# Attention with pooled queries, then a tanhshrink FFN: the sums of p in three instead of four rounds on TensorE

## The chip, the cores and the metric

One core of one Trainium2 chip runs the whole program in a single launch. The metric is the device time of the program in microseconds; the time before is the median of three runs.

## What is computed

The inputs are q, k and v of shape (8, 8, 1152, 64), that is 8 batches of 8 heads, and the two weights of an FFN, w_in (512 x 2048) and w_out (2048 x 512). The reference, cut to what matters:

```python
q_pool = q.reshape(B, H, S // 2, 2, D).mean(axis=3)
scores = scale * np.matmul(q_pool, k.transpose(0, 1, 3, 2))
scores = scores - np.max(scores, axis=-1, keepdims=True)
attn = np.exp(scores)
attn = attn / (np.sum(attn, axis=-1, keepdims=True) + 1e-09)
x = np.matmul(attn, v)            # then heads are put side by side: 4608 tokens x 512
h = x @ w_in
g = h - np.tanh(h)
out = g @ w_out
```

The change lies in np.sum(attn), the sum over the 1152 keys of the exponentials p.

## The kernel before, in words

The first half of the program is the attention, the second half the FFN. The attention goes over 32 pairs of heads (4 pairs in each of 8 batches). The two heads of a pair lie in the upper and the lower 64 partitions. A pair is worked in two halves of 288 pooled queries, and a half in 9 key tiles of 128 keys.

For one key tile TensorE makes the scores of both heads (`scores`, line 262): four products of 288 columns per head, with q and k split into a high and a low float32r part and a last product that adds minus the row maximum. ScalarE turns them into p (`p_f`, 128 x 2 x 288). After the ninth tile `pv` (line 285) multiplies all nine p tiles with v.

**The sums of p.** They are not taken on ScalarE but in two steps. GpSimd adds p tiles together (`z_part`, line 277): `z_groups` (line 449) names three groups of key tiles in each half, (0, 1, 2), (3, 4, 5) and (6, 7), and a group becomes one tile `z` with one addition fewer than it has members. The ninth p tile, key tile 8, is left alone. At the end of the second half `z_sums` (line 298) adds over the 128 keys of a tile with products of a 128 x 32 block of ones, in four rounds: first groups one and two, then the lone p tile, then group three. A round is four products, for two halves and two heads, each in its own 32 columns of the array. They go into the free half of the PSUM tile that the product with v fills.

**The row maxima for the next pair.** Between the score products TensorE also makes raw scores of high parts for the following pair (`max_part`, line 217, 15 of them in a pair, nine in the first half of a pair's time and six in the second, which ends with the sums), and VectorE reduces each to maxima (`mx`), 128 x 768 elements at a time. VectorE further makes the low part `lo` of q and k (line 213), and `nm`, `mt`.

**PSUM.** `banks()` (line 172) gives tiles of two banks from a pool of four. Scores, raw scores, the product with v and a small transposition all take their tile there, so that a tile comes free only after the ScalarE or VectorE instruction that reads it.

**The weights.** In the background of each pair one block of 512 weight columns is split into two float32r parts (`w_block`, line 347). That is five VectorE instructions on 128 x 512 elements (the trace names them `w<-w` and `w<-w_raw,w`; two of them are the last before a pair ends, a clip and a bitwise `and`, and three come at the middle of the pair), two of ScalarE and two of GpSimd (`w<-w,w` and `w_hl<-w,w_hl`).

**The order of the work** is written out by hand. Time is counted in units `u`, 36 for a pair (`U`) and 18 for a half (`G`); `add(u, f)` files a piece of work under a unit, and `run(u)` emits it there. Every engine keeps the order of emission (`InOrder`). Inside a pair, with r = u mod 36, the places that matter here are

- r = 35: the last group of `z_part`, `lo` of the pair after the next one, clip and `and` of the weight block; then `pv` and the sums;
- r = 36, that is r = 0 of the next pair: first the copies of the product and of the sums to SBUF, an early `max_part`, then the scores;
- r = 1: the `w_hl` subtraction of the weight block on GpSimd;
- r = 10: `query_sums` (line 201) on GpSimd, the sum `kq` of the two queries that are pooled, for the pair after the next one; its `hi` parts follow on ScalarE at r = 17;
- r = 22: the store of the maxima `m_dram` on SyncE's queue, which waits for VectorE; r = 28: the loads of q and k (`load`, line 185) for the pair after the next two, and the read of the maxima `mb`.

Pieces filed under the same unit keep the order in which they were filed; those of the loop at line 417 come ahead of what is filed while the program runs, so `query_sums` would come ahead of `w_hl` at the same unit, and `load` ahead of the store of the maxima.

```python
units = dict(load=-80, query_sums=-62, hi=-55, lo=-37, load_v=-30)
...
z_groups = {kts[-1]: kts for kts in ((0, 1, 2), (3, 4, 5), (6, 7))}
...
if r // 2 in z_groups:
    add(u + 1, z_part, hf, z_groups[r // 2])
```

Of the kernel before, what the change touches and what calls it, by code (L numbers as in the profile page):

```python
# [43 lines left out]
def kernel(  # L44
# [38 lines left out]
    ones = const.tile([P, 32], F32, name="ones")  # L83
# [51 lines left out]
    t, n = chunks.pop()  # L135
# [4 lines left out]
    with ExitStack() as actx:  # L140
# [10 lines left out]
        pe, act, dve, pool, sp = (InOrder(tc, e) for e in (nc.tensor, nc.scalar, nc.vector, nc.gpsimd, nc.sync))  # L151

        HQ = SQ // 2
# [23 lines left out]
        def add(u, f, *args, at=at):  # L177
            at.setdefault(u, []).append(lambda: f(*args))
# [106 lines left out]
        def pv(u, hf):  # L285

            w, ps = hf.w, banks()
            hf.o = ps[:, 0]
            for kt in range(KT):
                for h in range(2):  # L290
                    pe.matmul(hf.o[64 * h:64 * h + 64, 0:HQ], w.v[:, h, kt], hf.p[kt][:, h], start=(kt == 0),
                              stop=(kt == KT - 1), tile_position=(0, 64 * h))
            add(u + 1, o_out, w, hf, at=first)
            w.halves.append(hf)
            if hf.n == 1:
                z_sums(u, w, ps[:, 1])

        def z_sums(u, w, ps):

            parts = [[*hf.zs[:2], hf.p[-1], hf.zs[2]] for hf in w.halves]  # L300
            for g in range(4):
                for n in range(2):
                    for h in range(2):
                        r = 64 * h + 32 * n
                        pe.matmul(ps[r:r + 32, 0:HQ], ones, parts[n][g][:, h], start=(g == 0), stop=(g == 3), tile_position=(0, r))
            add(u + 1, z_out, u + 1, w, ps, at=first)

        def o_out(w, hf):
# [107 lines left out]

        for pi in range(n_pair):
            u = pi * U
            units = dict(load=-80, query_sums=-62, hi=-55, lo=-37, load_v=-30)
            row, steps = -19, (5, 11)  # L420

            spots = [x for half, us in ((-54, (2, 4, 8, 10, 12, 14, 16)), (-36, (2, 4, 8, 10, 14, 16)))
                     for x in [(early, half)] + [(at, half + i) for i in us]]
            if pi == 0:
                units.update(load=-70, query_sums=-62, hi=-60, lo=-41, load_v=-40)
                spots = [(at, -60 + i) for i in range(15)]
                row, steps = -43, (3, 4)
            if pi == 1:
                units.update(load=-104)
            add(u + units["load"], load, pi)  # L430
            add(u + units["query_sums"], query_sums, pi, dve if pi < 1 else pool)
            for c in range(0, KQ, SQ):
                add(u + units["hi"], hi_part, pi, c, c + SQ)
            add(u + units["lo"], lo_part, pi)
            for i, (when, x) in enumerate(spots):
                add(u + x, max_part, u + x, pi, i // 3, i % 3, at=when)
            add(u + units["load_v"], load_v, pi)
            add(u + row, max_rows, u + row, pi, steps)

        def run(u, at=at):  # L440

            while at.get(u):
                at[u].pop(0)()

        for u in range(min(at), 0):
            run(u, first)
            run(u, early)
            run(u)
        z_groups = {kts[-1]: kts for kts in ((0, 1, 2), (3, 4, 5), (6, 7))}
        for u in range(end + 60):  # L450
            run(u, first)
            run(u, early)
            n, r = divmod(u, G)
            if u < end and r % 2 == 0:
                if r == 0:
                    hf = Half()
# [18 lines left out]
    pe, pool, sp = (InOrder(tc, e) for e in (nc.tensor, nc.gpsimd, nc.sync))  # L475
# [81 lines left out]
    for ci, (t0, n) in enumerate(chunks):  # L557
        x_h, x_l, _ = xs
        po = []
        for fc in range(NF):  # L560
# [3 lines left out]
            load = []  # L564
            if ci + 1 < len(chunks):
# [3 lines left out]
                load = [xs[2][(fc - x) // 3][i] for i, x in ((3, 3), (0, 0), (1, 2), (2, 2)) if (fc - x) % 3 == 0 and 0 <= fc - x < 3 * NP]  # L569
            for f in load:  # L570
                f()
            g = hidden(x_h, x_l, n, fc)
# [44 lines left out]
```

## Time and profile before

| | before |
|---|---|
| median of 3 runs | 1643.94 us (1643.39 to 1645.49) |
| the profiled execution, whole | 1643.04 us |
| its span, first to last instruction | 1641.3 us |
| granted TensorE clock, mean over the span | 0.999 of 2.4 GHz |
| TensorE busy over the span | 1609.8 us (98%) |
| VectorE busy | 1319.6 us (80%) |
| ScalarE busy | 1023.9 us (62%) |
| GpSimd busy | 942.9 us (57%) |

The span is the profiler's time from the first to the last instruction of one execution. The execution itself took 1.74 us more, and 0.90 us less than the median. The attention fills about the first 843 us of the span, the FFN the rest. PE stands for TensorE's products, PEld for its weight loads, DVE for VectorE, ACT for ScalarE, POOL for GpSimd, and SPq for SyncE's queue of DMA issues. A line of 37 only says that the instruction went through the helper that keeps the order. Products are pipelined: a row of many shows from the start of the first to the end of the last, and their ends overlap with what starts next, so the distance of two starts is the better measure.

### The profile page before, as it was taken

The page shows a single profiled execution, that of the slowest core. Times are in us where ns is not written, and L with a number is a line of the kernel's source. Part 1 is how long each engine was busy: PE and PEld are TensorE (multiplying, and loading weights), DVE is VectorE, ACT ScalarE, POOL GpSimd, SP SyncE. Part 2 cuts the span into 40 slices and gives each one's busy share as a digit, 9 for nine tenths or more (in the row PEclk, how much of TensorE's full clock was granted, in tenths as well). Part 3 has the DMA queues.
Part 4 walks back from the last instruction along what each step waited for, and adds up shares of the span by engine and source line. Part 5 has one row for each costly group of instructions (what it writes and reads, how often), then busy time and mean ns, then how long its engine had stood idle before and what let it go on. Part 6 is the DMA issues. An engine that isn't in the chain of part 4 may idle for free.

```text
span 1641.3 us, 32231 instructions
## 1 busy us (share of the span) xinstructions
PE 1609.8 (98%) x12576; PEld 1245.2 (76%) x12576; DVE 1319.6 (80%) x1725; ACT 1023.9 (62%) x1865; POOL 942.9 (57%) x694
## 2 busy tenths in 40 slices
PE   5999999999999999999999999999999999999999
PEld 3667777777777777677778888888888888888898
DVE  7889888888898888888848677777777777777786
ACT  2655656556556565565566666666666666666786
POOL 2778778778787787877854343433434342423332
PEclk9999999999999999999999999999999999999999
DMA  3343444334433344343547110101011111000100
GB/s 141 120 138 108 126 127 136 125 108 138 135 115 125 121 141 126 108 130 133 183 146 268 39 36 21 48 26 52 26 47 31 39 39 39 26 33 20 32 22 27
DMA packets 72665, 147.86 MB, mean 90 GB/s; under 512 B 11136, under 2 KB 36672, under 8 KB 72512
## 3 DMA queue, kind: packets, MB, share of 16 engines
q1 hardware_dynamic: 72512, 145.80, 27.3%
q8 instruction: 99, 1.62, 0.4%
q14 instruction: 54, 0.44, 0.1%
HBM read 109.49 MB, written 36.27 MB: 89 GB/s over the span
## 4 chain that ended last, share of the span: by engine, by line
PE 85%; DVE 13%; issue 1%; ACT 0%; DMA 0%; DVEq 0%; ACTq 0%
PE ps L37 37%; PE ps_h L37 24%; PE ps_o L37 24%; DVE w L37 6%; DVE mx L37 6%; DVE nm L37 0%; DVE lo L37 0%; DMA q_n<-in_q_dram 0%; ACT hi L37 0%; DVE rec L37 0%; DVE kq L37 0%; ACT p_f L37 0%; DVEq L37 0%; ACT x L552 0%; ACT z_s L37 0%
## 5 line engine op out<-in xcount | busy, mean ns | idle before, releaser
L37 DVE TENSOR_REDUCE mx<-ps 128x2 f32<-128x768 f32 x480 | 434.3, 951 | 73.9 <-PE ps L37 73.7
L37 POOL TENSOR_TENSOR g_lo<-g_s,g_hi 128x512 fp32r<-128x512 f32 (+1 forms) x160 | 190.3, 1190 | 483.3 <-ACT g_hi L520 445.2
L37 ACT ACTIVATE p_f<-ps 128x576 f32<-128x576 f32 x576 | 361.7, 650 | 93.6 <-PE ps L37 79.3
L37 POOL TENSOR_TENSOR z<-p_f 128x576 f32<-128x576 f32 x192 | 280.0, 1459 | 154.1 <-ACT p_f L37 154.1
L37 PE MATMUL ps<-hi 64*128 64x288 f32 (+1 forms) x2112 | 316.7, 352 | 23.7 <-DVE mx L37 13.7
L37 PE MATMUL ps_h<-x,wi 128*128 128x512 f32 (+1 forms) x1440 | 318.3, 370 | 0.0
L37 PE MATMUL ps_o<-wo,g_hi 128*128 128x512 f32 x1008 | 311.5, 390 | 0.0
L37 PE MATMUL ps<-p_f,v 128*64 128x288 f32 x2304 | 293.5, 409 | 0.0
L37 PEld LDWEIGHTS ps_h<-x,wi 128*128 128x128 f32 x1440 | 253.1, 188 | 50.5
L37 PEld LDWEIGHTS ps<-hi 64*128 64x128 f32 x2112 | 194.4, 187 | 89.2 <-DVE mx L37 34.6
L37 PEld LDWEIGHTS ps<-p_f,v 128*64 128x64 f32 x2304 | 159.8, 137 | 113.7 <-ACT p_f L37 12.0
L509 ACT ACTIVATE g_u<-ps_h 128x512 f32<-128x512 f32 (+1 forms) x160 | 88.9, 556 | 236.3 <-PE ps_h L37 236.1
L514 DVE SCALAR_TENSOR_TENSOR ps_w<-g_u,ps_h 128x512 f32<-128x512 f32 (+1 forms) x160 | 103.1, 645 | 157.8 <-ACT g_t L510 157.2
L37 PEld LDWEIGHTS ps_o<-wo,g_hi 128*128 128x128 f32 x1008 | 187.6, 188 | 39.2
L37 POOL TENSOR_TENSOR z<-z,p_f 128x576 f32<-128x576 f32 x128 | 194.0, 1516 | 11.8 <-ACT p_f L37 1.9
L37 PE MATMUL ps_o<-wo,g_lo 128*128 128x512 f32 x504 | 196.2, 389 | 0.0
L37 PE MATMUL ps<-lo,hi 64*128 64x288 f32 x1152 | 170.8, 293 | 0.0
L37 PE MATMUL ps<-hi,lo 64*128 64x288 f32 x1152 | 170.7, 293 | 0.0
L37 PE MATMUL ps<-mb,ones_k 64*128 64x288 f32 x1152 | 170.2, 292 | 0.0
L37 ACT ACTIVATE o_s<-ps 128x288 f32<-128x288 f32 x64 | 26.3, 412 | 230.4 <-PE ps L37 230.4
L519 DVE COPY_PREDICATED g_s<-g_m,g_t 128x512 f32<-128x512 int32 (+1 forms) x160 | 115.0, 719 | 17.1 <-DVE g_s L518 0.9
L517 DVE SCALAR_TENSOR_TENSOR ps_w<-g_s,ps_w 128x512 f32<-128x512 f32 (+1 forms) x160 | 102.9, 643 | 16.6 <-DVE ps_w L516 0.5
(68 smaller groups left out, 2399.7 us busy)
## 6 DMA issues: line engine op xcount, KB each, us to landing
q_n<-in_q_dram SPq DMA_DIRECT2D x32, 576.0 KB
kq<-in_k_dram SPq DMA_DIRECT2D x32, 576.0 KB
v<-in_v_dram SPq DMA_DIRECT2D x32, 576.0 KB
x_dram<-o_s SPq DMA_DIRECT2D x32, 288.0 KB
out_dram<-o_s SPq DMA_DIRECT2D x34, 256.0 KB
w_raw<-in_moe_w_in_dram SPq DMA_DIRECT2D x16, 512.0 KB
wi_dram<-w_hl SPq DMA_DIRECT2D x16, 512.0 KB
w_raw<-in_moe_w_out_dram SPq DMA_DIRECT2D x16, 512.0 KB
```

The lines of the kernel that those rows point to most:

```text
L37: ins = self.tc.keep_in_program_order(f(*args, **kwargs))
L509: nc.scalar.activation(u, h, AF.Square)
L514: nc.vector.scalar_tensor_tensor(w, u, -P0, h, op0=ALU.add, op1=ALU.mult)
L517: nc.vector.scalar_tensor_tensor(w, s2, P2, w, op0=ALU.add, op1=ALU.mult)
L519: last = nc.vector.copy_predicated(s1, m.bitcast(I32), th).ins
```

## The change

The ninth p tile joins the third group on GpSimd, and the sums take three rounds of products with ones in place of four. The query sums of a pair are filed nine units sooner (r = 1 in place of r = 10; not for pairs 0 and 1), the loads of q and k six units sooner (r = 22 in place of r = 28; not for pairs 0 and 1).

```diff
         def z_sums(u, w, ps):
 
-            parts = [[*hf.zs[:2], hf.p[-1], hf.zs[2]] for hf in w.halves]
-            for g in range(4):
+            for g in range(3):
                 for n in range(2):
                     for h in range(2):
                         r = 64 * h + 32 * n
-                        pe.matmul(ps[r:r + 32, 0:HQ], ones, parts[n][g][:, h], start=(g == 0), stop=(g == 3), tile_position=(0, r))
+                        pe.matmul(ps[r:r + 32, 0:HQ], ones, w.halves[n].zs[g][:, h], start=(g == 0), stop=(g == 2),
+                                  tile_position=(0, r))
             add(u + 1, z_out, u + 1, w, ps, at=first)
...
-            units = dict(load=-80, query_sums=-62, hi=-55, lo=-37, load_v=-30)
+            units = dict(load=-86, query_sums=-71, hi=-55, lo=-37, load_v=-30)
...
             if pi == 1:
-                units.update(load=-104)
+                units.update(load=-104, query_sums=-62)
...
-        z_groups = {kts[-1]: kts for kts in ((0, 1, 2), (3, 4, 5), (6, 7))}
+        z_groups = {kts[-1]: kts for kts in ((0, 1, 2), (3, 4, 5), (6, 7, 8))}
```

## Rows read from the trace of the kernel before

**Rows 1.** One stretch: busy PE, PEld, DVE, ACT, POOL; clock, DMA share, GB/s.

```profile
400.00:500.00 100.00, 99.27 (x1102) 71.51 (x1100) 89.03 (x94) 60.16 (x107) 79.45 (x52) 1.00 0.40 126
```

**Rows 2.** The page's chain that ended last: share of the span by engine.

```profile
PE 85%; DVE 13%; issue 1%; ACT 0%; DMA 0%; DVEq 0%; ACTq 0%
```

**Rows 3.** Timeline of PE, end of a pair: start, duration (us), instruction.

```profile
391.38 0.94 PE L37 MATMUL ps<-z,ones 128*32 128x288 f32 x12
...
416.62 1.18 PE L37 MATMUL ps<-z,ones 128*32 128x288 f32 x16
417.62 0.67 PE L37 MATMUL ps<-p_f,ones 128*32 128x288 f32 x8
418.10 0.67 PE L37 MATMUL ps<-z,ones 128*32 128x288 f32 x8
418.70 0.57 PE L37 MATMUL ps<-hi 64*128 64x384 f32 x4
...
420.03 0.57 PE L37 MATMUL ps<-hi 64*128 64x384 f32 x4
420.43 0.30 PE L37 MATMUL ps<-lo,hi 64*128 64x288 f32 x2
```

**Rows 4.** Timeline of DVE, same pair's end (in brackets idle, releaser).

```profile
413.33 3.02 DVE L37 TENSOR_TENSOR lo<-kq,hi 128x1728 fp32r<-128x1728 f32 x1
416.27 1.49 DVE L37 TENSOR_SCALAR w<-w 128x512 f32<-128x512 f32 x1
...
417.79 0.43 DVE L37 TENSOR_SCALAR w<-w 128x512 int32<-128x512 int32 x1
419.18 0.96 DVE L37 TENSOR_REDUCE mx<-ps 128x2 f32<-128x768 f32 x1 [0.96 <-PE ps L37]
```

**Rows 5.** Timeline of POOL over the same end of a pair.

```profile
413.12 1.41 POOL L37 TENSOR_TENSOR z<-p_f 128x576 f32<-128x576 f32 x1
414.48 2.99 POOL L37 TENSOR_TENSOR w_hl<-w,w_hl 128x512 fp32r<-128x512 f32 x1
421.06 1.43 POOL L37 TENSOR_TENSOR z<-p_f 128x576 f32<-128x576 f32 x1 [3.59 <-ACT p_f L37]
```

**Rows 6.** Groups of instructions by line: count, busy us, mean ns, idle before.

```profile
L37 PE MATMUL ps<-p_f,ones 128*32 128x288 f32 x256 | 21.4, 406 | 0.0
```

**Rows 7.** Timelines of DVE and POOL at the start of the attention.

```profile
20.78 1.95 DVE L37 TENSOR_TENSOR lo<-kq,hi 128x1728 fp32r<-128x1728 f32 x1
...
32.41 1.63 DVE L37 TENSOR_SCALAR w<-w 128x512 f32<-128x512 f32 x1
...
34.07 1.50 DVE L37 TENSOR_SCALAR w<-w 128x512 int32<-128x512 int32 x1
...
32.01 1.74 POOL L37 TENSOR_TENSOR z<-p_f 128x576 f32<-128x576 f32 x1 [22.93 <-ACT p_f L37]
33.84 1.46 POOL L37 TENSOR_TENSOR z<-z,p_f 128x576 f32<-128x576 f32 x1
35.25 1.58 POOL L37 TENSOR_TENSOR kq<-q_n 128x576 f32<-128x576 f32 x1
```

**Rows 8.** Timeline of PE, the sums of pairs 1 and 2.

```profile
85.47 1.18 PE L37 MATMUL ps<-z,ones 128*32 128x288 f32 x16
...
112.53 1.18 PE L37 MATMUL ps<-z,ones 128*32 128x288 f32 x16
```

**Rows 9.** Timelines of POOL and PE, last pair but one.

```profile
819.73 1.86 POOL L37 TENSOR_TENSOR z<-p_f 128x576 f32<-128x576 f32 x1
821.55 1.73 POOL L37 TENSOR_TENSOR w_hl<-w,w_hl 128x512 fp32r<-128x512 f32 x1
...
820.08 1.18 PE L37 MATMUL ps<-z,ones 128*32 128x288 f32 x16
```

**Rows 10.** Timeline of SyncE's queue over the same pair.

```profile
407.44 0.34 SPq L37 DMA_DIRECT2D q_n<-in_q_dram  x1
...
421.22 1.24 SPq L37 DMA_DIRECT2D wo_dram<-w_hl  x1
```

## The prediction

> **What bounds the kernel now.** I read the table of busy time by stretch first. In a steady stretch of the attention TensorE is busy 99% of the time, VectorE 89% and GpSimd 79%, at the full granted clock [rows 1]. Three engines are nearly full, so it is not enough to know which one is fullest: the reader is to see that work moved from the first to the third has little room. The chain of waits says the same for the whole span: 85% of it lies on TensorE and 13% on VectorE [rows 2]. The place where they meet is the end of a pair, so I then read the timelines of three engines there. On TensorE the sums start at 416.62, and the lone p tile's round lasts from 417.62 to 418.10, 0.48 us, as does the next; the first product of the next pair starts at 418.70. From one pair's sums to the next it is 25.24 us [rows 3]. VectorE works through `lo`, clip and `and` until 418.22, and then waits 0.96 us for TensorE before it makes the first maxima of the next pair at 419.18 [rows 4]. GpSimd ends with the last group of p and `w_hl` at 417.47, and is then idle until 421.06 [rows 5].
>
> **The round that goes.** Four products a pair, two records each: 256 records in 32 pairs [rows 6]. By the distance of starts a round costs 0.48 us [rows 3], so 32 x 0.48 = 15.4 us leave TensorE's queue. That is the most the change can give.
>
> **The additions that come.** One in each half, 64 in all, of 1.43 us when nothing disturbs them [rows 5]: 92 us of GpSimd. A pair has 25.24 us, of which GpSimd is busy 79% [rows 1], 20.1 us; with 2 x 1.43 it is 22.9. They fit, but not without meeting VectorE.
>
> **Turns between VectorE and GpSimd.** With GpSimd idle `lo` takes 1.95 us [rows 7]; beside the additions it takes 3.02 [rows 4]. Rows 7 show how this works, by the ends of the instructions. The addition issued at 32.01 ends at 33.75; clip, issued at 32.41, ends at 34.04, 0.29 later; the addition issued at 33.84 ends at 35.30, 1.26 after clip; `and`, issued at 34.07, ends at 35.57, 0.27 after that; `kq`, issued at 35.25, ends at 36.83, again 1.26 later [rows 7]. The two engines take strict turns, each instruction waits for the whole of the other's, and a waiting GpSimd instruction goes in between clip and `and`. At the end of the steady pair it is the same: the addition of tiles 6 and 7 ends at 414.53, `lo` at 416.35 (1.82 later), `w_hl` at 417.47 (1.12 later), clip at 417.76; then GpSimd has nothing left and `and` runs alone [rows 4, 5]. The maxima read PSUM and are not held up.
>
> The Trainium skill says so as a rule (SBUF — State Buffer, "SBUF: two separate sides"): the pair of ports that the two engines share is held for the whole instruction by whichever starts first, and the other is blocked fully. It speaks against this change; the trace agrees, with the 3.02 for 1.95 above. Without it the rival at 1632.7 below would be the forecast.
>
> **The end of a pair after the change.** GpSimd now has three instructions where it had two: the ninth addition, `kq` (moved here from r = 10), `w_hl`. I lay them out in turns from 414.53, with the durations above: `lo` to 416.35; ninth addition 1.27, to 417.62; clip 0.29, to 417.91; `kq` 1.27, to 419.18; `and` 0.28, to 419.46. VectorE issues some 0.08 before the end of its last instruction (clip starts at 416.27 [rows 4]), so the first maxima start at 419.39 and end, after 0.96, at 420.35. Before, they ended at 420.14 [rows 4].
>
> TensorE starts the next pair 0.48 sooner, at 418.22. But PSUM has four tiles: raw scores, scores, scores, raw scores take them, and the fifth, the third scores, needs the first raw scores' tile, after its maxima. Before, that one's first products lie in the row at 420.03, some 0.13 ahead of the next pair of products at 420.43, so at 420.30, 0.16 after the maxima [rows 3]. Now they start at 420.35 + 0.16 = 420.51: 0.21 later than before, not 0.48 sooner. So the maxima become what ends last, and TensorE's gain is spent waiting. Part of the 0.21 is regained, since the tiles behind wait for ScalarE, which got its scores sooner. The ends for an ordinary pair are +0.21 (nothing regained) and -0.24 (half of the 0.48 gets through after all, by a last group that starts sooner against the sums). I take 0, which lies within 0.1 of half the 0.21. For 29 pairs that is 0, between -7.0 and +6.1 us.
>
> The ninth addition itself, done at 417.62, is needed by the third round's second half at 416.62 + 1.00 + 0.24 = 417.86: hidden, with 0.24 to spare. If that cover goes, the wait for the maxima (0.7 us from 419.8, when TensorE would reach that tile) still covers as much. The first half's ninth addition takes the place that `kq` left between the groups; VectorE has three weight instructions there and waits for two additions as before: 0, at most one turn of 1.27 either way in a pair that has slipped, which I leave inside the ends above.
>
> **Two pairs that are not ordinary.** The pair between 85.47 and 112.53 takes 27.06 us, 1.82 over a steady one [rows 8]: a second weight block is split there, and the whole of its VectorE work stands in front of the first maxima. So late maxima do reach TensorE. With a longer list on VectorE each GpSimd instruction added gets its turn: ninth addition and `kq`, 2 x 1.27 = 2.5, less about 0.5 of TensorE's own gain: +2.0 us (ends 0 and +2.5). At the last pair but one GpSimd is late already: the addition of tiles 6 and 7 ends at 821.59, after the sums began at 820.08, and `w_hl` at 823.28 [rows 9]. The ninth addition will stand where `w_hl` stood and end at some 823.4, where the sums need it at 820.08 + 1.24 = 821.32: a wait of 2.1, less 0.48, +1.6 us (ends 0 and +2.1). The last pair has no maxima and keeps its round: -0.4.
>
> **Moved steps.** `load` issues two DMAs (q and k) some 10 us sooner: it stood right behind the store of the maxima, at 407.44, which waits for VectorE, and will follow the weights' store, which lies at 421.22 and so, one pair of 25.24 earlier, near 396.0 [rows 10]. Its buffers were last read by `lo`, which is done at 416.35, so it does not hold the store of the maxima behind it, and the read of the maxima no longer queues behind its data. Nobody waits for either now: 0. `kq` at r = 1 finds its data there, and `hi` needs it 16 units later: 0. `w_hl`, behind `kq`, ends at 419.46 + 1.12 = 420.6: its store is issued at 421.22 [rows 10] and the next addition starts at 421.06 [rows 5], so 0, with 0.5 us of cover; beyond that the next group of p would be late, which is not needed before the pair's end.
>
> **Sum.** 0 + 2.0 + 1.6 - 0.4 = +3.2 us on the profiled execution's 1643.04, and on the median of 1643.94: 1647.1. The attention alone changes.
>
> **Rivals.** (a) TensorE sets the pace and the maxima are not what ends last: `and` gets ahead of `kq`, ends near 418.3, and the first maxima start when TensorE gives them. Then 30 pairs give 0.48 each, -14.4, with +2.0, +1.6 and -0.4 as above: -11.2, 1632.7. For it: VectorE's idle 0.96 before these maxima [rows 4]. Against it: `and` lost just this turn in rows 7. (b) The plain reading, with no meeting at all: -15.4, 1628.5. TensorE's 99% speaks for it [rows 1], the turns against. The Trainium skill (Perfetto Trace Analysis, "Identifying the Most-Contended Engine") calls the busy share of matmuls a poor measure and takes occupancy for VectorE; by it VectorE is the fuller one, and the gain of (b) would be none; the chain's 13% lends it some weight. (c) On the slow side: GpSimd's last group falls one turn behind, the ninth addition ends at 417.62 + 1.27 = 418.9, and the third round waits 1.0. The next pair then starts at 419.25, 0.55 later than before; in 30 pairs +16.5, with +3.2: 1663.6. It decides once the second half's groups start more than 0.24 us later against the sums than now. GpSimd's 22.9 of 25.24 us speaks against it, its waits in turns for it. That the change does not do what it says is hardly possible: the records of a round are simply gone.
>
> **How the numbers follow.** The forecast has 0.66, (a) 0.18, (b) 0.06, (c) 0.10. The forecast's own range is 1640 to 1654, from the ends of the ordinary pairs and of the two others. Down to (a) it is 1632 to 1654; (b), (c) and some of the forecast's tail stay out. A measurement of this kernel can tell some 0.2%, 3.3 us. Faster by more, below 1640.7: (a), (b) and 0.04 of the forecast, 0.28. Slower, above 1647.2: (c) and not quite half of the forecast, 0.41. Within: 0.31.
>
> **What would show it.** In the profile after, a round fewer (768 records of `z,ones`, none of `p_f,ones`); `and` long (about 1.5 in place of 0.43) with `kq` beside it; the first maxima of a pair with no idle time before them, and PE waiting for `mx` at the third scores; a steady pair between 25.0 and 25.45 us; 823.4 for the ninth addition of the last pair but one. A steady pair of 24.8 with `and` at 0.43 would show (a); PE waiting for `z` in every pair, (c). The forecast is wrong above all if the maxima are late and TensorE does not wait, or if the groups of p start at another time against the sums.

## The result, and the profile after

The changed kernel takes 1646.97 us (median of nine runs, 1646.07 to 1649.17), the kernel before on the same chip 1643.39 (nine runs, 1642.74 to 1645.49): a ratio of 1.0024, interval 1.0015 to 1.0032. The forecast was 1647.1. The profiled execution took 1646.16 us with a span of 1644.3, against 1643.04 and 1641.3. TensorE was busy for 1600.4 us of that span, 9.4 less than before, GpSimd for 1035.1, 92.2 more, which is what 64 additions of 1.43 us were to cost. The round is gone (768 records of `z,ones`, none of `p_f,ones`), and the time grew all the same.

First the busy time of the stretch that [rows 1] show before:

```profile
400.00:500.00 100.00, 97.92 (x1074) 70.77 (x1072) 93.54 (x94) 60.34 (x107) 91.16 (x60) 1.00 0.38 125
```

TensorE fell from 99.27 to 97.92%, VectorE rose from 89.03 to 93.54% although it got no instruction, GpSimd from 79.45 to 91.16%. The chain that ended last, as in [rows 2]:

```profile
PE 71%; DVE 25%; POOL 1%; issue 1%; ACT 0%; DMA 0%; DVEq 0%; ACTq 0%; POOLq 0%
PE ps_h L37 24%; PE ps_o L37 24%; PE ps L37 23%; DVE mx L37 12%; DVE w L37 8%; DVE lo L37 5%; POOL z L37 1%; DMA q_n<-in_q_dram 0%; DVE nm L37 0%; ACT hi L37 0%; ACT p_f L37 0%; POOL kq L37 0%; POOL w_hl L37 0%; DVE rec L37 0%; DVEq L37 0%
```

Before, the second line read:

```profile
PE ps L37 37%; PE ps_h L37 24%; PE ps_o L37 24%; DVE w L37 6%; DVE mx L37 6%; DVE nm L37 0%; DVE lo L37 0%; DMA q_n<-in_q_dram 0%; ACT hi L37 0%; DVE rec L37 0%; DVE kq L37 0%; ACT p_f L37 0%; DVEq L37 0%; ACT x L552 0%; ACT z_s L37 0%
```

VectorE's share of the chain doubled from 13 to 25%, and the second lines say with what: maxima, weights and `lo`. The groups of instructions (count, busy us, mean ns, idle before) show it from the other side, first before, then after:

```profile
L37 DVE TENSOR_REDUCE mx<-ps 128x2 f32<-128x768 f32 x480 | 434.3, 951 | 73.9 <-PE ps L37 73.7
...
L37 PEld LDWEIGHTS ps<-hi 64*128 64x128 f32 x2112 | 194.4, 187 | 89.2 <-DVE mx L37 34.6
...
L37 DVE TENSOR_SCALAR w<-w 128x512 int32<-128x512 int32 (+1 forms) x96 | 106.0, 1104 | 5.3 <-DVE w L37 0.9
```

```profile
L37 DVE TENSOR_REDUCE mx<-ps 128x2 f32<-128x768 f32 x480 | 434.4, 950 | 39.1 <-PE ps L37 38.6
...
L37 PEld LDWEIGHTS ps<-hi 64*128 64x128 f32 x2112 | 193.6, 188 | 101.4 <-DVE mx L37 53.6
...
L37 DVE TENSOR_SCALAR w<-w 128x512 int32<-128x512 int32 (+1 forms) x96 | 142.3, 1482 | 6.5
```

The maxima are as long as before, but VectorE's idle time ahead of them fell from 73.9 to 39.1 us: it comes late more often. What TensorE's loads of the `hi` weights wait for maxima rose from 34.6 to 53.6 us. Clip and the `and` instructions, the last line, cost 142.3 us in place of 106.0: longer by waiting, since their work is the same.

At the end of a steady pair the timelines of the three engines (start, duration; beside [rows 3 to 5]) read:

```profile
419.20 1.70 PE L37 MATMUL ps<-z,ones 128*32 128x288 f32 x24
420.83 0.58 PE L37 MATMUL ps<-hi 64*128 64x384 f32 x4
...
422.94 0.40 PE L37 MATMUL ps<-hi 64*128 64x288 f32 x2 [0.44 <-DVE mx L37]
...
415.90 3.01 DVE L37 TENSOR_TENSOR lo<-kq,hi 128x1728 fp32r<-128x1728 f32 x1
418.83 3.19 DVE L37 TENSOR_SCALAR w<-w 128x512 f32<-128x512 f32 x2
421.94 1.81 DVE L37 TENSOR_REDUCE mx<-ps 128x2 f32<-128x768 f32 x2
...
417.17 3.00 POOL L37 TENSOR_TENSOR z<-z,p_f 128x576 f32<-128x576 f32 x1
420.13 1.60 POOL L37 TENSOR_TENSOR kq<-q_n 128x576 f32<-128x576 f32 x1
421.70 1.45 POOL L37 TENSOR_TENSOR w_hl<-w,w_hl 128x512 fp32r<-128x512 f32 x1
```

From the start of the sums, the next pair's first product comes at +1.63 (before +2.08): TensorE has its 0.45 us. The ninth addition, blocked while `lo` runs, ends at +0.97; `kq` runs between clip and `and`, which together take 3.19 us; the first maxima start at +2.74 with no idle time before them, and the third scores wait 0.44 us for their tile. So nearly all of the gain is spent there.

In the ordinary pairs the sums start 25.04 to 25.28 us apart in most, 24.76 to 24.91 in a few, and 25.55 to 25.81 where a batch opens. From the third sums (115.96) to the thirtieth (798.60) 27 pairs take 682.64 us, against 684.55 before (112.53 to 797.08).

### The profile page after: what moved, and what is told of

It is laid out like the page before. It is cut to its first block, busy times and chain, and to the rows that moved or that the text cites. A ratio compares the mean times of both kernels' runs of the same rounds, so it can differ in the third digit from the quotient of the medians.

```text
span 1644.3 us, 31920 instructions
## 1 busy us (share of the span) xinstructions
PE 1600.4 (97%) x12320; PEld 1240.5 (75%) x12320; DVE 1354.1 (82%) x1725; ACT 1024.0 (62%) x1865; POOL 1035.1 (63%) x758
## 4 chain that ended last, share of the span: by engine, by line
PE 71%; DVE 25%; POOL 1%; issue 1%; ACT 0%; DMA 0%; DVEq 0%; ACTq 0%; POOLq 0%
PE ps_h L37 24%; PE ps_o L37 24%; PE ps L37 23%; DVE mx L37 12%; DVE w L37 8%; DVE lo L37 5%; POOL z L37 1%; DMA q_n<-in_q_dram 0%; DVE nm L37 0%; ACT hi L37 0%; ACT p_f L37 0%; POOL kq L37 0%; POOL w_hl L37 0%; DVE rec L37 0%; DVEq L37 0%
## 5 line engine op out<-in xcount | busy, mean ns | idle before, releaser
L37 DVE TENSOR_REDUCE mx<-ps 128x2 f32<-128x768 f32 x480 | 434.4, 950 | 39.1 <-PE ps L37 38.6
L37 POOL TENSOR_TENSOR z<-z,p_f 128x576 f32<-128x576 f32 x192 | 330.5, 1721 | 18.2 <-ACT p_f L37 3.4
L37 POOL TENSOR_TENSOR z<-p_f 128x576 f32<-128x576 f32 x192 | 276.2, 1438 | 28.3 <-ACT p_f L37 27.3
L37 PEld LDWEIGHTS ps<-hi 64*128 64x128 f32 x2112 | 193.6, 188 | 101.4 <-DVE mx L37 53.6
L37 PEld LDWEIGHTS ps_o<-wo,g_hi 128*128 128x128 f32 x1008 | 187.6, 188 | 39.1
L37 DVE TENSOR_SCALAR w<-w 128x512 int32<-128x512 int32 (+1 forms) x96 | 142.3, 1482 | 6.5
```

Source lines behind the costliest of these rows:

```text
L37: ins = self.tc.keep_in_program_order(f(*args, **kwargs))
```

## The experiments

The mean pair in the table is taken over the same 27 pairs of each profiled run, and each ratio is to the kernel before as it ran beside that experiment. An edit is made to the kernel named ahead of it.

| kernel | median us | ratio to before, interval | mean pair us |
|---|---|---|---|
| before | 1643.39 | 1 | 25.35 |
| after | 1646.97 | 1.0024 (1.0015 to 1.0032) | 25.28 |
| e1 before, three rounds over eight p tiles | 1630.83 | 0.9920 (0.9905 to 0.9934) | 24.90 |
| e2 e1, with both moves of the change | 1636.47 | 0.9956 (0.9941 to 0.9971) | 25.14 |
| e3 after, with four rounds | 1649.74 | 1.0035 (1.0021 to 1.0050) | 25.38 |
| e4 after, query sums back at r = 10 | 1665.35 | 1.0132 (1.0117 to 1.0147) | 25.95 |
| e5 after, clip and `and` sooner | 1633.54 | 0.9940 (0.9928 to 0.9953) | 24.91 |
| e6 e5, with query sums back | 1647.09 | 1.0023 (1.0013 to 1.0033) | 25.40 |
| e7 after, loads back | 1646.52 | 1.0021 (1.0012 to 1.0030) | 25.26 |
| e8 before, the two moves alone | 1640.75 | 0.9984 (0.9975 to 0.9993) | 25.24 |
| e9 e5, with a third buffer | 1632.87 | 0.9933 (0.9918 to 0.9947) | 24.91 |
| e10 before, clip and `and` sooner | 1641.63 | 0.9989 (0.9979 to 0.9999) | 25.35 |
| e11 e9, with the extra block moved | 1632.64 | 0.9931 (0.9917 to 0.9945) | 24.93 |

### What the round is worth: e1, e2, e3

**e1**, on the kernel before: the lone tile's round is dropped and nothing is added.

```diff
-            for g in range(4):
+            for g in range(3):
...
-    parts[n][g][:, h] ... stop=(g == 3)
+    w.halves[n].zs[g][:, h] ... stop=(g == 2)
```

> Three rounds, and the ninth p tile is left out of the sums altogether; query sums and loads stand where they did before. So TensorE's round is gone and nothing has come to GpSimd. Theory (turns: the gain is real, and is lost to late maxima because GpSimd instructions stand between VectorE's last ones of a pair): the full gain, 0.48 us in every pair, a steady pair of 24.76, some 15 us less than before (1628 to 1630). Rival (VectorE is the bound in any case, a round of TensorE is worth nothing): within 3 us of before.

1630.83 us: 12.6 less than the 1643.44 beside it, just short of the 1628 to 1630 expected. Its 27 pairs take 0.46 us less each, nearly all of the 0.48 that a round costs, so in an ordinary pair the round by itself is worth its whole length.

**e2** has the changed kernel's places for query sums and loads as well; against the changed kernel only the ninth additions are missing.

```diff
-        z_groups = {kts[-1]: kts for kts in ((0, 1, 2), (3, 4, 5), (6, 7, 8))}
+        z_groups = {kts[-1]: kts for kts in ((0, 1, 2), (3, 4, 5), (6, 7))}
```

> As the last one (the ninth p tile is in no sum), but with the query sums at r = 1 and the loads sooner, as in the changed kernel. GpSimd has no more work than before; only the query sum now stands where VectorE's clip and `and` are. Theory (turns): `w_hl` no longer follows the last group directly, `and` waits for a whole GpSimd instruction, the first maxima come some 1.1 us later than in the first of these runs, and most of the gain is lost: 3 to 6 us less than before (1638 to 1641), a steady pair of about 25.2. Rival (GpSimd's additional 92 us are what eats the gain): they are not there, so all of it stays, 15 us less than before.

1636.47 us, a little better than forecast. The moves eat 5.6 of the 12.6 us, with no addition there yet (e7 below finds no cost in the loads, which leaves `kq` at r = 1): it gets its turn between clip and `and`, which take 3.05 us in this trace (3.19 after, 1.95 in e1), and the ordinary pairs are 25.12 long in place of 24.76. From e2 to the changed kernel the ninth additions cost another 10.5 us; in the profiled runs 3.9 us of that lie in the 27 pairs and 5.1 in the two intervals ahead of them and the two behind. So the rival is half right: the additional work costs most, but the moved `kq` costs without it.

**e3** is the change with the fourth round kept (the lone tile is multiplied as before, and added by GpSimd too).

```diff
-            for g in range(3):
+            for g in range(4):
...
+    [*w.halves[n].zs[:2], w.halves[n].p[-1], w.halves[n].zs[2]][g][:, h] ... stop=(g == 3)
```

> All of the change but the round that goes: the ninth p tile is added on GpSimd and still has its own round, so it is counted twice in the sums. Theory (turns): TensorE's round hides in the wait for the maxima, so this is hardly slower than the changed kernel, 1 to 4 us above it and 4 to 8 us above before; steady pairs of 25.27. Rival (TensorE sets the pace, and the addition costs what the round gives): 15 us above the changed kernel, some 18 above before.

1649.74 us, 2.8 over the changed kernel; the intervals just overlap, and the 27 pairs of the profiled runs differ by 2.7. The same round that is worth 12.6 us when it is taken from the kernel before is worth 2.8 here: the rest is hidden behind a VectorE that is late in any case.

### What the moved steps are worth: e4, e7, e8

**e4** puts `query_sums` back to r = 10, all else as after.

```diff
-            units = dict(load=-86, query_sums=-71, hi=-55, lo=-37, load_v=-30)
+            units = dict(load=-86, query_sums=-62, hi=-55, lo=-37, load_v=-30)
...
```

> The changed kernel with the query sums at r = 10 again (loads still sooner). Theory (turns): the end of a pair is better, since `w_hl` alone follows the ninth addition, but the middle gets one GpSimd instruction more among VectorE's three weight instructions and the groups of the second half slip; together worse than the changed kernel, by 2 to 6 us, with periods that alternate between some 24.8 and 26.2. Rival (where the query sum stands is of no account, GpSimd's total is): within 2 us of the changed kernel.

1665.35 us, 18.4 over the changed kernel: the direction was right, the size missed by far. Of the 18.1 us that its 27 pairs lose, 15.05 lie in the seven that open a batch (194.58 against 179.53 us). The busy time of one of them by stretch, and VectorE's and TensorE's timeline in its middle:

```profile
255.00:265.00 10.00, 8.27 (x79) 5.79 (x77) 9.41 (x12) 5.35 (x11) 9.23 (x8) 0.95 0.30 82
265.00:275.00 10.00, 10.00 (x98) 7.36 (x99) 8.58 (x9) 4.42 (x7) 9.09 (x6) 0.88 0.26 99
```

```profile
257.22 1.45 DVE L37 TENSOR_SCALAR w<-w 128x512 int32<-128x512 int32 x1
258.70 1.77 DVE L37 SCALAR_TENSOR_TENSOR w<-w_raw,w 128x512 f32<-128x512 uint16 x1
260.40 1.39 DVE L37 TENSOR_SCALAR rec<-rec 128x36 f32<-128x36 f32 x1
...
262.12 0.90 DVE L37 TENSOR_REDUCE mx<-ps 128x2 f32<-128x768 f32 x1
...
263.07 0.59 PE L37 MATMUL ps<-hi 64*128 64x384 f32 x4 [1.73 <-DVE mx L37]
```

`rec`, of 36 columns, takes 1.39 us; in the changed kernel, at 256.27, it takes 0.18. With `kq` and the first half's ninth addition both ahead of them, GpSimd's groups of p reach these VectorE instructions one after the other and each takes a turn. The maxima behind come late, TensorE waits 1.73 us, and after that it does not run at full speed (0.95 and 0.88 in the first fence). All seven pairs that open a batch have this wait, of 1.73 to 1.75 us, but TensorE falls to half speed behind it in only three of them; these take 28.5 us and the remaining four 27.2. In the pairs that open no batch GpSimd's last group comes late by up to 0.8 us, and TensorE feels it: its weight loads wait 14.8 us for `z` between 130 and 800 us, in 23 waits, and not once in the same stretch of the changed kernel. But those 20 pairs together lose only 3 us.

**e7** puts only the loads back.

```diff
-            units = dict(load=-86, query_sums=-71, hi=-55, lo=-37, load_v=-30)
+            units = dict(load=-80, query_sums=-71, hi=-55, lo=-37, load_v=-30)
```

> The changed kernel with the loads of q and k at r = 28 again. By the step of the prediction that gives them no cost or gain: within 1 us of the changed kernel. Rival (loads so near to the query sums at r = 1, or the read of the maxima behind them, hold something up): 5 us or more above it.

1646.52 us, 0.45 less than after, with intervals that overlap: the loads' place costs nothing and gives nothing that shows.

**e8** makes only the two moves, in the kernel before.

```diff
-            units = dict(load=-80, query_sums=-62, hi=-55, lo=-37, load_v=-30)
+            units = dict(load=-86, query_sums=-71, hi=-55, lo=-37, load_v=-30)
...
```

> The kernel before with the two moves alone: query sums at r = 1, loads sooner, four rounds and eight tiles added as before. Theory (turns): the middle of a pair loses a GpSimd instruction, the end gets one, with TensorE's round still there to cover the later maxima: 0 to 3 us less than before (1640 to 1643.5). Rival (the moves by themselves cost what the change lost): 5 us or more above before.

1640.75 us, 2.45 less than the 1643.20 beside it. Of the 2.9 us that its 27 pairs gain, 2.7 lie in the seven that open a batch, which fall from some 25.63 to the 25.24 of the others. So the two moves are good for the kernel before as well, most likely through `kq` out of the middle (the loads by themselves were put back only in the changed kernel, e7); TensorE's fourth round covers what `kq` does at the pair's end.

### What ends last at a pair's end: e5, e10, e6

**e5**: in the changed kernel clip and `and` come two units sooner, r = 33, so ahead of the last group and of `lo`; the last raw maxima of the pair come behind them.

```diff
-                          (30, lambda: ts(whole(t[0]), whole(t[0]), -top, top, op0=ALU.max, op1=ALU.min)),
-                          (30, lambda: ts(t[1], t[0], -0x80000000, None, op0=ALU.bitwise_and)),
+                          (28, lambda: ts(whole(t[0]), whole(t[0]), -top, top, op0=ALU.max, op1=ALU.min)),
+                          (28, lambda: ts(t[1], t[0], -0x80000000, None, op0=ALU.bitwise_and)),
```

> The changed kernel, with the clip and the `and` of the weight block two units sooner (r = 33 in place of 35), so that they stand ahead of the last maxima and of `lo` and no longer between `lo` and the next pair's first maxima. All work is the same. Theory (turns at the end of a pair are what eats the gain): the first maxima wait for nothing but TensorE, the round's 0.48 us come through in every ordinary pair (24.76 to 24.8), some 11 to 13 us less than before: 1630 to 1633. Rival (the ninth additions cost what they cost wherever VectorE's instructions stand, since each of the 64 blocks VectorE once): within 3 us of the changed kernel, 1644 to 1650.

1633.54 us, 13.4 less than after and 9.7 less than before, just outside the 1630 to 1633 expected. The same end of a pair:

```profile
412.72 1.66 PE L37 MATMUL ps<-z,ones 128*32 128x288 f32 x24
414.32 0.58 PE L37 MATMUL ps<-hi 64*128 64x384 f32 x4
...
408.56 0.98 DVE L37 TENSOR_SCALAR w<-w 128x512 f32<-128x512 f32 x1
409.99 1.09 DVE L37 TENSOR_SCALAR w<-w 128x512 int32<-128x512 int32 x1 [0.46 <-DVE w L37]
411.00 0.95 DVE L37 TENSOR_REDUCE mx<-ps 128x2 f32<-128x768 f32 x1
411.87 2.29 DVE L37 TENSOR_TENSOR lo<-kq,hi 128x1728 fp32r<-128x1728 f32 x1
414.80 0.96 DVE L37 TENSOR_REDUCE mx<-ps 128x2 f32<-128x768 f32 x1 [0.64 <-PE ps L37]
...
412.31 3.14 POOL L37 TENSOR_TENSOR kq<-q_n 128x576 f32<-128x576 f32 x1
```

Now `lo` is VectorE's last instruction before the maxima, and it is `kq` that waits for `lo` (3.14 us). VectorE idles 0.64 us again before the first maxima, which start at +2.08 from the sums in place of +2.74, and the pairs are 24.76 to 24.78 us long (25.20 to 25.48 where a batch opens), as in e1. Two instructions that nobody needs at that moment stood in front of 13 us.

**e10** makes this very edit, 28 for 30 in the same two lines, in the kernel before.

> The kernel before, four rounds, with nothing but clip and `and` of the weight block two units sooner. My theory: the 13 us that this edit gave in the changed kernel are the round's, set free once the first maxima come early enough; in the kernel before TensorE's fourth round covers most of the delay of the maxima, and what the edit frees is at most the 0.1 to 0.2 us per pair by which the maxima still came late: 1638 to 1643, a steady pair 25.1 to 25.25. Rival: the edit is worth 10 us or more by itself, whatever the round does, and the round gives nothing even then: 1630 to 1635, a steady pair 24.8 to 24.9.

1641.63 us, 1.6 less. Its 27 pairs take 684.44 us, as the 684.55 before: nothing in an ordinary pair, although VectorE idles 1.25 us there now. So the edit sets free no time of its own; what it gives in e5 is the round's.

**e6** is e5 with e4's edit (`query_sums=-62`).

> As the last one, but with the query sums at r = 10 again. Theory (turns): with no VectorE instruction of the weights at the end of a pair, the place of the query sums matters at the middle only. If what cost 18 us in the run with the query sums back is that GpSimd falls behind at the middle and the last group then loses its turn to `lo`, that stays, and this is again 10 us or more slower than the last one (1640 to 1655). If it came from the end of the pair (clip and `and` there), it is gone: 1630 to 1634.

1647.09 us, 13.5 over e5. Of the 13.2 us in its 27 pairs, 12.65 lie in the seven that open a batch (189.90 against 177.25). So most of what `kq` at r = 10 costs lies in the middle of a pair. With clip and `and` out of the way it costs 4.9 us less than e4's 18.4, so they have a smaller part in it.

### The pair with two weight blocks: e9, e11

In the changed kernel the interval from the second sums to the third grew by more than forecast. TensorE's timeline there, and its stretch:

```profile
85.28 1.66 PE L37 MATMUL ps<-z,ones 128*32 128x288 f32 x24
...
92.21 0.61 PE L37 MATMUL ps<-hi 64*128 64x288 f32 x2 [3.67 <-DVE mx L37]
92.61 0.44 PE L37 MATMUL ps<-lo,hi 64*128 64x288 f32 x2
92.86 0.44 PE L37 MATMUL ps<-hi,lo 64*128 64x288 f32 x2
...
97.66 0.32 PE L37 MATMUL ps<-hi,lo 64*128 64x288 f32 x2
97.81 0.30 PE L37 MATMUL ps<-mb,ones_k 64*128 64x288 f32 x2
```

```profile
90.00:100.00 10.00, 7.79 (x72) 7.37 (x73) 7.05 (x8) 4.37 (x8) 7.27 (x6) 0.66 0.83 284
```

After 3.67 us without a product the next ones start 0.24 us apart, until 97.66; elsewhere the same products start 0.13 apart. The granted clock of the stretch is 0.66, where it was 1.00 before, behind a wait of 1.09 us:

```profile
90.31 0.40 PE L37 MATMUL ps<-hi 64*128 64x288 f32 x2 [1.09 <-DVE mx L37]
```

```profile
90.00:100.00 10.00, 9.69 (x103) 7.09 (x103) 9.04 (x11) 7.21 (x13) 9.26 (x7) 1.00 0.54 166
```

In e8, with the moves alone, TensorE waits 2.08 us here, the clock of this stretch is 0.83, and the interval is 28.73 us in place of 27.06.

**e9** is e5 with a third buffer for the tile that `and` writes. With two, `and` in e5 waited 5.38 us here for the `w_hl` subtraction of an earlier block, since three are under way in this pair alone:

```profile
85.43 0.43 DVE L37 TENSOR_SCALAR w<-w 128x512 int32<-128x512 int32 x1 [5.38 <-POOL w_hl L37]
```

```diff
-                t[:] = [wp.tile([P, WB], I32, name=f"w_{i}", bufs=1 + (i < 2)) for i in range(3)]
+                t[:] = [wp.tile([P, WB], I32, name=f"w_{i}", bufs=(2, 3, 1)[i]) for i in range(3)]
```

> The changed kernel with clip and `and` of the weight block two units sooner, and a third buffer for the tile that `and` writes. With two buffers `and` waited 5.38 us (80.0 to 85.4) for the w_hl subtraction of the block before it, in the one pair in which three blocks are under way, and the maxima of the next pair came late: that pair took 30.17 us, and the granted clock was 0.83 between 90 and 100 us. My theory: that wait alone makes this pair long. Without it VectorE is some 4 us earlier, the pair takes 26 to 27 us, no clock is lost in 90 to 100 us, and the time is 3 to 4.5 us under the 1633.5 of the same kernel with two buffers: 1629 to 1630.5. Rival: VectorE simply has too much to do in this pair, since two weight blocks meet in it; then the wait turns into work and the gain is under 1.5 us: 1632 to 1633.5, with the pair still over 28.5.

1632.87 us: 0.7 less than e5, and the pair still takes 28.78. The theory fell: the wait turned into turns with GpSimd, and TensorE is still idle for 2.71 us:

```profile
89.63 0.40 PE L37 MATMUL ps<-hi 64*128 64x288 f32 x2 [2.71 <-DVE mx L37]
```

**e11** also moves the middle instructions of the extra block out of that pair's end.

```diff
+            mid = 40 if u == 23 else 48
...
-                          (48, lambda: stt(t[1], t[0], 3, t[1], op0=ALU.logical_shift_left, op1=ALU.bitwise_or)),
+                          (mid, lambda: stt(t[1], t[0], 3, t[1], op0=ALU.logical_shift_left, op1=ALU.bitwise_or)),
...
-                          (50, lambda: pool.tensor_tensor(whole(t[1]), whole(t[1]), whole(t[2]), op=ALU.add)),
+                          (mid + 2, lambda: pool.tensor_tensor(whole(t[1]), whole(t[1]), whole(t[2]), op=ALU.add)),
```

> The kernel with clip and `and` two units sooner and the third buffer, in which the three middle VectorE instructions of the extra weight block (and the GpSimd addition behind them) also come eight units sooner, ahead of the second half's last key tiles instead of at the end of the pair. With the third buffer alone that pair took 28.78 us, TensorE stood 2.71 us still for the first maxima at 89.6, and the products between 91.1 and 94.4 then started 0.24 us apart in place of 0.13 (granted clock 0.83 over 90 to 100). My theory: 3.4 us of VectorE in front of the first maxima make the wait, and the wait is what the clock fell behind; with the work elsewhere both go, the pair takes 24.8 to 25.8 us, the granted clock is 1.00 in 90 to 100 us, and the time is 3 to 4 us under 1632.9: 1629 to 1630. Rival 1: the pair's length comes from VectorE having more work in it than it has time, wherever it stands; then the stall moves to another place of the pair or the one before it and the gain is under 1 us. Rival 2: the clock falls there whatever TensorE does (a burst of transfers at the same time); then the gain is 1 to 2 us, with 0.83 still in the row of 90 to 100 us.

1632.64 us, the same as e9 within the intervals, so rival 1 holds for the gain: that pair takes 26.37 us and its clock is 1.00, but the pair before it grew from 25.75 to 27.28, with TensorE waiting 1.10 us for `mx` in it and 0.94 for `z` in the sums at its end. Rival 2 fell: without the long wait the clock stays up, although more is transferred in that stretch (DMA share 0.91, against 0.63 in e9).

Part of the rest went where nothing had been edited. e9 and e11, last pair but one, TensorE's timeline and stretch; first e9:

```profile
810.85 0.68 PE L37 MATMUL ps<-z,ones 128*32 128x288 f32 x4 [1.78 <-POOL z L37]
...
812.22 0.30 PE L37 MATMUL ps<-lo,hi 64*128 64x288 f32 x2
812.36 0.29 PE L37 MATMUL ps<-hi,lo 64*128 64x288 f32 x2
```

```profile
810.00:820.00 10.00, 9.15 (x106) 7.08 (x108) 3.92 (x3) 6.84 (x13) 8.21 (x6) 1.00 0.22 84
```

and e11:

```profile
810.79 0.68 PE L37 MATMUL ps<-z,ones 128*32 128x288 f32 x4 [1.71 <-POOL z L37]
...
812.26 0.44 PE L37 MATMUL ps<-lo,hi 64*128 64x288 f32 x2
812.50 0.44 PE L37 MATMUL ps<-hi,lo 64*128 64x288 f32 x2
```

```profile
810.00:820.00 10.00, 9.21 (x94) 7.79 (x96) 3.66 (x3) 6.91 (x13) 7.79 (x6) 0.83 0.22 84
```

The same wait, 1.78 and 1.71 us, is followed by the full clock in e9 and by the half in e11, and the pair takes 23.09 or 24.49 us: 1.4 us of difference that no edit made. In e4 to e7 the wait there is 1.70 or 1.71 us too, and the pair takes 23.02 to 23.04.

## Why the prediction was right, and where not

The sum of the forecast against what the starts of the sums show:

| term | forecast | measured |
|---|---|---|
| up to the second sums | 0 | -0.19 |
| pair with two weight blocks | +2.0 (0 to +2.5) | +3.62 |
| 27 ordinary pairs | 0 (-7.0 to +6.1 for 29 pairs) | -1.91 |
| the two intervals to the last sums | +1.6 (0 to +2.1) | +1.54 |
| behind the last sums | -0.4 | 0.0 |
| sum | +3.2 | +3.1 |

The range's upper end of 1654 takes every term to its end, the lower one of 1640 only the ordinary pairs; with the two others at 0 as well it would be 1636.5. Nothing hangs on it here.

**The mechanism held.** The turns at a pair's end came in the order and with the times of the forecast: ninth addition done 0.97 us after the sums began (1.00 forecast), first maxima at +2.74 (2.77), next pair at +1.63 (1.60). The third scores come at +3.74 from the sums, 0.15 us later than before (forecast 0.21 later). Before, they started at 420.21 and not at the 420.30 that the prediction took from a merged row:

```profile
420.21 0.39 PE L37 MATMUL ps<-hi 64*128 64x288 f32 x2
```

That slip of 0.09 stands on both sides of its difference and cancels. That the maxima, and not TensorE, end last is shown and not only read: e5 takes two VectorE instructions out of that place and 13.4 us appear, while e10 finds hardly any of them as long as the fourth round stands. With e1 (12.6 us gained without the additions), e2 (5.6 of them lost to the moves), the 10.5 us of the ninth additions behind it and e3 (the round worth 2.8 us with them), that settles where the 15.4 us went. The Trainium skill's rule on the shared port (SBUF — State Buffer, "SBUF: two separate sides"), weighed in the prediction, agrees with `and` and `kq` in turns here, and with `rec` of 1.39 us for 0.18 in e4 (the last section has an instruction that was not held up).

**Rivals.** (a) and (b), 1632.7 and 1628.5, did not happen; e5 at 1633.54 is what (a) looks like once `and` does get ahead of `kq`. (c), the groups of p falling behind, did not happen in the change. e4 shows its sign, waits for `z`, but also that (c) had the wrong place: GpSimd's lateness costs most in the middle of a pair, through VectorE's turns there, where the prediction put it at the pair's end.

**Where sizes were off.** Ordinary pairs gained 0.07 us each, and the forecast took 0: of the -0.24 to +0.21 it allowed, a little more of TensorE's gain gets through than was taken. All of it lies in the pairs behind those that open a batch (24.76 to 25.05 us in six of seven, against 25.24).

The one term outside its bounds is the pair with two weight blocks. The step was "With a longer list on VectorE each GpSimd instruction added gets its turn: ninth addition and `kq`, 2 x 1.27 = 2.5, less about 0.5 of TensorE's own gain: +2.0 us (ends 0 and +2.5)". That much is right: the third scores come at +6.93 from the sums, and before at 90.31 - 85.47 = 4.84, so 2.09 later. But the rest of the interval takes 23.75 us in place of 22.22, another 1.5, with half speed in the rows: the products that start from 92.21 to 97.66, 5.45 us, took 3.20 before. A wait was priced at its own length, and the slow stretch behind it at nothing.

**The last pair but one.** Its ninth addition ends 3.16 us after the sums began (3.3 forecast), and TensorE's timeline has the wait in the row at 824.70:

```profile
821.48 1.65 PE L37 MATMUL ps<-z,ones 128*32 128x288 f32 x20
824.70 0.68 PE L37 MATMUL ps<-z,ones 128*32 128x288 f32 x4 [1.57 <-POOL z L37]
```

The interval to the last sums is 22.90 in place of 21.24 us, +1.66 for the +1.6, and the one before it 0.12 shorter. The last pair's own 0.4 did not come through: from the last sums to the end both spans take 799.9 us.

**Moved steps.** The loads' 0 is confirmed by e7. For `kq` the forecast's 0 meant that its data is there in time, which held, and it was silent about why it had to be made: the ninth addition of the first half was put down at 0 because it "takes the place that `kq` left". e4 shows what that cover is worth, 18.4 us.

So the total came within 0.2 us of the forecast partly by luck: two errors, -1.9 and +1.6, cancelled, and the 1643.94 from which the forecast started lies 0.55 above the median of the nine runs, from which the change costs 3.6 us. e5 is faster than both kernels by a single number, 28 for 30 in two lines; e9 and e11 add nothing that can be measured.

## What to carry to other kernels

Work moved from a full engine to one that shares a resource with a third is paid by the third: lay out the turns at the place where the engines meet before counting the gain. When an expected gain does not come, look for what stands in front of the instruction that now ends last and is not needed there; here that was two instructions, worth 13 us after the change and 1.6 before it. Price a stall of TensorE with the slow products behind it, and look at such a change pair by pair, since a total that agrees can hide terms that don't.

## What the runs showed of the hardware

**The clock behind a wait.** After TensorE stood still for 3.67 us the products started 0.24 us apart in place of 0.13 for 5.4 us, which is its 1.2 GHz level, and the granted clock of that 10 us stretch was 0.66. After 2.71 us (e9) it was 0.83, after 2.08 us (e8) 0.83, after 1.71 us 0.83 in e11 and after 1.78 us 1.00 in e9. e4 shows both outcomes in one trace: the wait of 1.73 us at 263.07 is followed by half speed, the same wait in another pair that opens a batch is not:

```profile
159.83 0.58 PE L37 MATMUL ps<-hi 64*128 64x384 f32 x4 [1.74 <-DVE mx L37]
```

```profile
160.00:170.00 10.00, 10.00 (x110) 7.31 (x110) 9.48 (x9) 5.05 (x8) 9.25 (x6) 1.00 0.37 122
```

So a wait of some 1.7 us may or may not cost a further 1.3 to 1.4 us. The Trainium skill (TensorE: Matmul & The Clock Gate, "Part 1: The HAM clock gate") takes the half rate for the default that activity lifts; the rows agree in that full speed comes back while products run, at 97.66. That the changed kernel's runs spread from 1646.1 to 1649.2 us with mean granted clocks between 0.995 and 0.999 would fit such chances, but only one of them has a trace here, so this is argued and not shown.

**A short instruction can lose a whole turn.** `rec`, 128 x 36 elements, took 1.39 us in e4 where GpSimd was busy with a 128 x 576 addition, and 0.18 where it was not: what it lost was the rest of the other engine's instruction, not a share of its own length. Not every VectorE instruction is held up: the reciprocal of the same 128 x 36 elements right behind it, at 261.83, took only 0.38 us although a GpSimd addition was under way from 261.71 to 262.97. The reductions from PSUM took the same beside GpSimd (0.95 us at 411.00 in e5, with an addition under way) and without it (0.96 at 419.18 in [rows 4]).
